# Soft-capped attention followed by a maxout layer on one core: early loads in whole rows, an earlier second stage, the last sum block and the normalisation on VectorE

## The chip, the cores and the metric

One Trainium2 chip, one of its cores. The metric is the device time of one execution in microseconds, lower is better. Times of single instructions come from one profiled execution, recorded by the hardware profiler. The kernel is written in Bass with an order of work laid out by hand: each engine runs its instructions in the order in which the program emits them, and waits on semaphores where data or a buffer is not ready.

## The reference

Attention over 8 batches, 12 heads, 448 positions, 64 columns, with a soft cap on the scores, then a layer with two products and a maximum, and an output product:

```python
scores = scale * np.matmul(q, k.transpose(0, 1, 3, 2))
scores = cap * np.tanh(scores / cap)
scores = scores - np.max(scores, axis=-1, keepdims=True)
attn = np.exp(scores)
attn = attn / (np.sum(attn, axis=-1, keepdims=True) + 1e-09)
attn_out = np.matmul(attn, v)
x = attn_out.transpose(0, 2, 1, 3).reshape(B * S, H * D)     # 3584 x 768
g = np.maximum(x @ w1, x @ w2)                               # 3584 x 1024
return g @ w_out                                             # 3584 x 768
```

The kernel writes the maximum as max(a, b) = relu(a - b) + b: it forms w1 - w2 once (`wd_sb`), and folds the "+ b" part into a premultiplied matrix w2 @ w_out (`wm_sb`). So the second stage is relu(x (w1 - w2)) @ w_out + x (w2 w_out). Preparing `wd_sb` and `wm_sb` is called M here.

## The kernel before

**Tiles.** Two heads make a pair, 48 pairs in all, six to a batch. Three pairs make a group (16 groups, g = 0 to 15), which is the unit of loading. Two pairs make a quad (24 quads, t = 0 to 23), which is the unit of the main loop. Within a quad, ab = 0 or 1 names the pair. Index i = 2t, 2t + 1 counts half quads. The 448 positions of keys are three blocks of 128 and a left block of 64; the left blocks of a pair's two heads are put together as one 128-row block.

**Attention.** `scores(t, p)` makes the scores of a quad in four parts p and puts tanh behind each on ScalarE; `ex(t, p)` is the exp on ScalarE (part 2 holds the left blocks). `pv(t, ab)` multiplies exp with v: six matmuls into `ps` for the full blocks, and one for the left one. With ab = 1 it also makes the sums of exp over the keys in `ss`, with matmuls by a matrix of ones: two 64-column ones for the left block (L340, `ones2`), and 32-column ones for the rest (L347). For quads below `NS` = 5, L347 runs over all three blocks (12 matmuls); from quad 5 on, `add` has summed the three blocks on VectorE first (`esum`, L319 and L321), and four matmuls do. VectorE copies `ps` to `U[t]` (L351, three buffers) and `ss` to `st` (L354).

**The sums' way.** `st` goes by DMA to a 32 x 56 tile `sums` (L357); `invert` takes the reciprocal on VectorE (L363) and writes it to DRAM (L365, `rec_d`); `spread` broadcasts it from there into `rec_b` (L371, two DMAs); `normalize` multiplies U by it into `xT` (L383), on GpSimd, once per pair. In the loop, spread and normalize of quad t - 2 stand in quad t.

**Loads.** Groups 0 to 3 (`NT` = 4) load k and q in rows of seven positions, 1792 bytes, and are transposed on TensorE (`transposes`); their v comes in packets of 768 and 256 bytes in four DMAs. Later groups are cast to bf16 on GpSimd (`cast`) and turned by a transposing DMA on SyncE's queue (`cross`, L268). Raw tiles have two buffers per operand. `load_w1` (SyncE), `load_w2` and `load_wo` (GpSimd, with a cast on the way) bring the weights.

**The fill.** Work of M (`turn_w2`, `premultiply`) and of the second stage (`moe(b)`, one per batch) stands in `fill_q` as generators that yield after each matmul. `F(n)` lets n of these matmuls run between the attention's steps. moe(b) has 48 first-stage matmuls (L396, 448 columns, eight groups of six, each ended by a relu on VectorE, L400), then 14 per half output tile (L408 and L411, 384 columns, ended by a copy on VectorE, L415), 84 or 112 of them. The `mm` tile, which all of the fill writes, has two PSUM buffers. F slots per quad are 44, from quad 8 on 48.

**What sets the order.** The list `todo[i]` holds loads, casts and transposing DMAs of each half quad, run by `extra(i)`; the loop over t writes out everything else. M starts at half quad `MS` = 3, `subtract` (w1 - w2, L214) is placed by MS too, and moe(0) enters the queue at the start of quad 5. SyncE's queue takes all input loads after the weights, the sums' three DMAs, the transposing DMAs and the outputs, in the order of emission.

Of the kernel before, what the change touches and what calls it, by code (L numbers as in the profile page):

```python
# [10 lines left out]
def kernel(  # L11
# [21 lines left out]
    P = 128  # L33
# [80 lines left out]
    def load(g, what, n0=0, n1=L):  # L114
        b, p = divmod(g * L, NP)
        h0, h1 = 2 * (p + n0), 2 * (p + n1)
        src = {"k": k, "q": q, "v": v}[what]
        t, m, l = raw_of(g, what)
        if g < NT and what == "v":

            x = rows(src, b, h0, h1).rearrange("(h r) c -> r h c", r=64)
            for a in range(2):
                nc.sync.dma_start(
                    out=m[64 * a : 64 * a + 64, 2 * n0 : 2 * n1, :], in_=x[:, :, NJ * D * a : NJ * D * (a + 1)]
                )
            for par in range(2):
                nc.sync.dma_start(
                    out=l[64 * par : 64 * par + 64, n0:n1, :], in_=x[:, par::2, 2 * NJ * D :]
                )
            return  # L130
        if g < NT:
            nc.sync.dma_start(
                out=t[:, n0 * S : n1 * S].rearrange("p (n c) -> p n c", c=S),
                in_=rows(src, b, h0, h1).rearrange("(n p) c -> p n c", p=P),
            )
            return
        nc.sync.dma_start(
            out=m[:, 2 * n0 : 2 * n1, :],
            in_=src[b, h0:h1, 0 : NJ * P, :].rearrange("h (p j) d -> p h (j d)", j=NJ),
        )  # L140
        if what == "q":
            nc.sync.dma_start(
                out=l[half(b), 2 * n0 : 2 * n1, :],
                in_=src[b, h0:h1, NJ * P : S, :].rearrange("h p d -> p h d"),
            )
        else:
            for par in range(2):
                nc.sync.dma_start(
                    out=l[64 * par : 64 * par + 64, n0:n1, :],
                    in_=src[b, h0 + par : h1 : 2, NJ * P : S, :].rearrange("h p d -> p h d"),  # L150
                )

    def cast(eng, g, what, n0=0, n1=L):

        b = g * L // NP
        x, m, l = raw_of(g, what)
        if what == "v":
            eng.tensor_copy(  # L158
                vp[g % 2][:, 2 * n0 : 2 * n1, :, :].rearrange("p h j d -> p h (j d)"), m[:, 2 * n0 : 2 * n1, :]
            )  # L160
            for par in range(2):
                r = slice(64 * par, 64 * par + 64)
                eng.tensor_copy(vl[g % 2][r, n0:n1, r], l[r, n0:n1, :])
            return
        if g < NT:

            x = x[:, n0 * S : n1 * S].rearrange("p (n c) -> p n c", c=S)
            if what == "q":
                eng.tensor_copy(flat(g)[:, n0:n1, Q0 : Q0 + S], x)
                return  # L170
            eng.tensor_copy(flat(g)[:, n0:n1, : NJ * P], x[:, :, : NJ * P])
            for par in range(2):
                r = slice(64 * par, 64 * par + 64)
                eng.tensor_copy(kf[g % 2][r, n0:n1, 3, r], x[r, :, NJ * P :])
            return
        o = b % 2 if what == "q" else 0
        t = (kf if what == "k" else qf)[g % 2]
        eng.tensor_copy(
            t[:, n0:n1, o : o + NJ, :].rearrange("p n j (h d) -> p n h j d", h=2),
            m[:, 2 * n0 : 2 * n1, :].rearrange("p (n h) (j d) -> p n h j d", h=2, d=D),  # L180
        )
        if what == "q":
            eng.tensor_copy(
                t[half(b), n0:n1, 3 * (1 - o), :],
                l[half(b), 2 * n0 : 2 * n1, :].rearrange("p (n h) d -> p n (h d)", h=2),
            )
        else:
            for par in range(2):
                r = slice(64 * par, 64 * par + 64)
                eng.tensor_copy(t[r, n0:n1, 3, r], l[r, n0:n1, :])  # L190
# [120 lines left out]
    def add(t, ab, step):  # L311
# [3 lines left out]
        if t not in esum:  # L315
            esum[t] = att.tile([P, 4, S], bf16, name="esum")
        d = esum[t][:, 2 * ab : 2 * ab + 2, :]
        if step == 0:
            nc.vector.tensor_add(d, e_of(t, ab, 1 if ab else 0), e_of(t, ab, 2 if ab else 1))  # L319
        else:  # L320
            nc.vector.tensor_add(d, d, e_of(t, ab, 0 if ab else 2))  # L321
# [3 lines left out]
    def pv(t, ab):  # L325
# [10 lines left out]
                )  # L336
        if ab:
            ss = pv_psum.tile([P, 512], f32, name="ss")
            for m in range(2):
                nc.tensor.matmul(  # L340
                    ss[64 * m : 64 * m + 64, :S], ones2, expo[t, 2][:, m, :], start=True, stop=False
                )
# [1 line left out]
            for j in range(nj):  # L344
                for m in range(4):
                    x = e_of(t, m // 2, j)[:, m % 2, :] if t < NS else esum[t][:, m, :]
                    nc.tensor.matmul(ss[32 * m : 32 * m + 32, :S], ones, x, start=False, stop=(j == nj - 1))  # L347
        nc.tensor.matmul(ps[:, :S], vl[g % 2][:, n, :], expo[t, 2][:, ab, :], start=False, stop=True)  # L348
        if ab == 0:
            U[t] = upool.tile([P, 2, S], f32, name="u", bufs=3)  # L350
        nc.vector.tensor_copy(U[t][:, ab, :], ps[:, :S])  # L351
        if ab:
            st = upool.tile([P, S], f32, name="st", bufs=1)
# [20 lines left out]

    xT = {}

    def normalize(t, ab, eng=nc.gpsimd):
        i = 2 * t + ab
        b, hp = divmod(i, NP)
        if i % (2 * NP) == 0:  # L380
            xT[b // 2] = xpool.tile([P, NP, 2 * S], bf16, name="xT")
        cs = slice((b % 2) * S, (b % 2 + 1) * S)
        eng.tensor_mul(xT[b // 2][:, hp, cs], U[t][:, ab, :], rec[t][:, ab, :])  # L383


    gT = {}
# [61 lines left out]
    NL = N // L  # L448
    NS = 5
    todo = [[] for _ in range(N)]  # L450

    def at(i, f, *a):
        todo[i].append((f, a))

    for g in range(2, NL):
        if g < NT:
            e = 0 if g == 2 else 1
            at(3 * g - 6 + e, load, g, "k")
            at(3 * g - 6 + e, load, g, "q")
            at(3 * g - 4 + e, load, g, "v")  # L460
            at(3 * g - 4, cast, nc.gpsimd, g, "k")
            at(3 * g - 4, cast, nc.gpsimd, g, "q")
            at(3 * g - 2, cast, nc.gpsimd, g, "v")
        else:
            e = 3 * g - g % 2
            at(e - 8, load, g, "k")
            at(e - 8 + g % 2, load, g, "q")
            at(e - 6, cast, nc.gpsimd, g, "k")
            at(e - 6, cast, nc.gpsimd, g, "q")
            at(e - 4, cross, g)  # L470
            at(e - 4, load, g, "v")
            at(e - 2, cast, nc.gpsimd, g, "v")
    at(1, load, 1, "v")
    at(2, cast, nc.gpsimd, 1, "v")
    for c, i in enumerate((3, 3, 4, 5, 6, 7)):
        todo[i].insert(c if i == 3 else 0, (load_w1, (c,)))
    MS = 3

    fill_const(nc.vector, 0)
    load(0, "k", 0, 1)  # L480
# [3 lines left out]
    load(1, "k")  # L484
    load(1, "q")
    load(0, "v")
    cast(nc.vector, 0, "k", 0, 1)
    cast(nc.gpsimd, 0, "q", 0, 1)
    fill_const(nc.gpsimd, 1)
    transposes(0)  # L490
    cast(nc.vector, 0, "k", 1, L)
    cast(nc.vector, 0, "q", 1, L)
# [7 lines left out]
    ex(0, 2)  # L500
    scores(0, 3)
    transposes(2)
    cast(nc.vector, 0, "v")
    cast(nc.gpsimd, 1, "k")
    cast(nc.gpsimd, 1, "q")
    for f in range(0, FC, 2):
        load_wo(f)
    for c in range(3):
        load_w2(c)
    for c in range(3, KC):  # L510
        load_w2(c)

    def weights(i):
# [9 lines left out]
    for t in range(NQ):  # L523
# [1 line left out]
        more = t + 1 < NQ  # L525
        more8 = 1 if t >= 8 and more else 0
        weights(i)
        if t % 3 == 2 and t > 2:
            fill_q.append(moe(t // 3 - 1))
        if more:  # L530
            scores(t + 1, 0)
        ex(t, 3)
        F(2)
        add(t, 0, 1)
        F(2)
        if i + 3 < NT * L:
            transposes(i + 3)
        F(5 + more8 if more else 0)
        if t > 4:
            spread(t - 2)  # L540
        extra(i)
        F(6 if more else 3)
        if more:
            scores(t + 1, 1)
            ex(t + 1, 0)
        pv(t, 0)
        F(8 + more8)
        F(3 if more else 0)
        if MS < i <= MS + KC:
            subtract(i - MS - 1)  # L550
        if t > 4:
            normalize(t - 2, 0)
            normalize(t - 2, 1)
        if more:
            scores(t + 1, 2)
            ex(t + 1, 1)
        weights(i + 1)
        if i + 4 < NT * L:
            transposes(i + 4)
        F(2 + more8 if more else 0)  # L560
        add(t, 1, 0)
        F(4 if more else 2)
        add(t, 1, 1)
        F(2 if more else 0)
        if t > 4:
            invert(t - 1)
        elif t > 1:
            spread(t - 2)
        extra(i + 1)
        F(3 + more8 if more else 0)  # L570
        if more:
            scores(t + 1, 3)
            ex(t + 1, 2)
        pv(t, 1)
        F(4)
        if more:
            add(t + 1, 0, 0)
        F(3 if more else 0)
        if 0 < t < 5:
            invert(t - 1)  # L580
        if 1 < t < 5:
            normalize(t - 2, 0)
            normalize(t - 2, 1)
        if MS < i + 1 <= MS + KC:
            subtract(i - MS)
    F(6)
    spread(NQ - 2)
    F(10)
    invert(NQ - 1)
    F(16)  # L590
    spread(NQ - 1)
    normalize(NQ - 2, 0)
    normalize(NQ - 2, 1)
    F(30)
    normalize(NQ - 1, 0)
    normalize(NQ - 1, 1)
    fill_q.append(moe(B - 1))
    F(10 ** 9)
# [33 lines left out]
```

## Time and profile before

| | us |
|---|---|
| median of 13 runs | 378.46 |
| lowest and highest of them | 375.65, 382.05 |
| the profiled execution | 377.91 |
| its span, first to last instruction | 376.1 |
| granted TensorE clock, mean | 0.986 |

What engine groups cost in that execution (busy us, count, mean ns):

| group | busy | count | mean |
|---|---|---|---|
| ScalarE exp L303, 1792 columns or 896 | 144.8 | 96 | 1509 |
| ScalarE tanh L296 | 124.2 | 144 | 914 |
| TensorE second stage L411, L396, L408 | 85.5, 79.2, 66.6 | 448, 384, 336 | 326, 354, 326 |
| GpSimd normalize L383, 128x448 | 58.5 | 48 | 1240 |
| VectorE esum L319, L321, 128x896 | 28.2, 29.5 | 38, 38 | 742, 777 |
| VectorE relu L400, 128x448 | 39.0 | 64 | 615 |
| TensorE sums of the left block L340 | 8.7 | 48 | 361 |

A matmul's duration here overlaps the next one's, so busy sums of TensorE overstate its work; distances between starts are the better measure. A row "engine line waited for" of a wait table gives the total, the times and the longest in microseconds.

### The profile page before, as it was taken

How to read it: one execution, taken by the hardware profiler on the slowest of the kernel's cores; microseconds unless marked ns; L12 is line 12 of the kernel's file. 1: busy time of each engine (PE TensorE's matmuls, PEld its weight loads, DVE VectorE, ACT ScalarE, POOL GpSimd, SP SyncE). 2: the span in 40 equal slices, each digit the busy share in tenths (PEclk: the TensorE clock that was granted, in tenths of full speed). 3: DMA queues.
4: the chain of work that ended last, by engine and by line, in shares of the span. 5: the costliest groups of instructions: out<-in, count | busy, mean ns of one | idle time of the engine just before them, and what ended most of it. 6: DMA issues, size and time to landing. Idle time of an engine off the chain costs nothing.

```text
span 376.1 us, 6549 instructions
## 1 busy us (share of the span) xinstructions
PE 348.2 (93%) x2492; PEld 167.7 (45%) x2492; DVE 201.5 (54%) x348; ACT 281.6 (75%) x265; POOL 148.8 (40%) x188
## 2 busy tenths in 40 slices
PE   4677887898999999999999999999999999999996
PEld 2223443342454445444444445444444454555563
DVE  4222474565665576465636755466557666533421
ACT  4999996695999989998898889988988996000000
POOL 3833137536554245615372546343643402420000
PEclk9998998998999999999999999999999999999999
DMA  7999999987779996989697959896979232332022
GB/s 269 271 217 223 300 284 234 206 159 148 209 198 203 227 252 174 211 218 250 198 245 194 250 164 248 245 243 167 249 191 244 53 113 99 108 93 84 2 84 85
DMA packets 104464, 71.56 MB, mean 190 GB/s; under 512 B 58224, under 2 KB 99440, under 8 KB 104432
## 3 DMA queue, kind: packets, MB, share of 16 engines
q1 hardware_dynamic: 102480, 67.99, 70.8%
q0 software_dynamic: 1952, 3.15, 4.5%
q8 instruction: 19, 0.31, 0.4%
q14 instruction: 13, 0.11, 0.1%
HBM read 53.48 MB, written 11.18 MB: 172 GB/s over the span
## 4 chain that ended last, share of the span: by engine, by line
PE 71%; DMA 10%; DVE 6%; ACT 4%; SPq 4%; issue 2%; POOL 2%; POOLq 0%; DVEq 0%; ACTq 0%
PE mm L411 18%; PE mm L396 17%; PE mm L408 14%; PE pv L334 7%; PE s L295 7%; PE pv L348 3%; DMA rec_b<-rec_d 3%; DMA vr<-in_v_dram 3%; DMA qkT<-kqf 2%; PE ss L347 2%; ACT tanh L296 2%; ACT expo L303 2%; PE s L290 2%; DMA qr<-in_q_dram 2%; DVE u L351 1%
## 5 line engine op out<-in xcount | busy, mean ns | idle before, releaser
L296 ACT ACTIVATE tanh<-s 128x896 bf16<-128x896 f32 x144 | 124.2, 914 | 28.8 <-PE s L295 27.6
L303 ACT ACTIVATE expo<-tanh 128x1792 bf16<-128x1792 bf16 (+1 forms) x96 | 144.8, 1509 | 0.1
L383 POOL TENSOR_TENSOR xT<-u,rec_b 128x448 bf16<-128x448 f32 x48 | 58.5, 1240 | 102.2 <-DMA rec_b<-rec_d 93.5
L411 PE MATMUL mm<-wo_sb,gT 128*128 128x384 bf16 x448 | 85.5, 326 | 0.0
L396 PE MATMUL mm<-xT,wd_sb 128*128 128x448 bf16 x384 | 79.2, 354 | 2.3 <-POOL xT L383 1.3
L351 DVE COPY u<-pv 128x448 f32<-128x448 f32 x48 | 29.9, 623 | 89.5 <-PE pv L348 78.9
L408 PE MATMUL mm<-wm_sb,xT 128*128 128x384 bf16 x336 | 66.6, 326 | 0.7 <-DVE gT L400 0.7
L411 PEld LDWEIGHTS <-gT 128*128 128x128 bf16 x448 | 43.3, 98 | 30.5 <-issue 2.6
L415 DVE COPY osb<-mm 128x384 f32<-128x384 f32 x56 | 30.9, 553 | 43.9 <-PE mm L411 43.8
L396 PEld LDWEIGHTS <-wd_sb 128*128 128x128 bf16 x384 | 37.2, 98 | 38.0 <-issue 5.4
L295 PE MATMUL s<-qkT 64*128 64x448 bf16 x288 | 43.9, 375 | 10.3 <-ACT tanh L296 3.6
L400 DVE TENSOR_SCALAR gT<-mm 128x448 bf16<-128x448 f32 x64 | 39.0, 615 | 17.2 <-PE mm L396 17.0
L408 PEld LDWEIGHTS <-xT 128*128 128x128 bf16 x336 | 32.5, 98 | 24.0 <-issue 2.7
L334 PE MATMUL pv<-expo,vp 128*64 128x448 bf16 x288 | 38.1, 374 | 0.0
L158 POOL CAST vp<-vr 128x1152 bf16<-128x1152 f32 x15 | 18.0, 1199 | 48.4 <-DMA vr<-in_v_dram 26.9
L321 DVE TENSOR_TENSOR esum<-esum,expo 128x896 bf16<-128x896 bf16 x38 | 29.5, 777 | 1.5
L319 DVE TENSOR_TENSOR esum<-expo 128x896 bf16<-128x896 bf16 x38 | 28.2, 742 | 0.0
L298 ACT ACTIVATE tanh<-s 128x896 bf16<-128x896 f32 x24 | 22.0, 916 | 5.2 <-PE s L290 4.7
L295 PEld LDWEIGHTS <-qkT 64*128 64x128 bf16 x288 | 9.6, 95 | 36.1 <-issue 30.2
L334 PEld LDWEIGHTS <-vp 128*64 128x64 bf16 x288 | 12.5, 111 | 21.9 <-issue 17.0
L232 PE MATMUL mm<-wo_sb,w2T 128*128 128x384 bf16 x96 | 18.4, 326 | 1.4 <-DVE qkT L264 1.4
L348 PE MATMUL pv<-expo,vl 128*128 128x448 bf16 x48 | 17.7, 369 | 0.0
(56 smaller groups left out, 222.2 us busy)
## 6 DMA issues: line engine op xcount, KB each, us to landing
rec_b<-rec_d SPq DMA_DIRECT2D x48, 224.0 KB
kr<-in_k_dram SPq DMA_DIRECT2D x12, 576.0 KB
qr<-in_q_dram SPq DMA_DIRECT2D x12, 576.0 KB
vr<-in_v_dram SPq DMA_DIRECT2D x12, 576.0 KB
out_dram<-osb SPq DMA_DIRECT2D x17, 384.0 KB
out_dram<-osb SPq DMA_DIRECT2D x22, 192.0 KB
osb<-in_moe_w_dram SPq DMA_DIRECT2D x6, 512.0 KB
vr<-in_v_dram SPq DMA_DIRECT2D x8, 288.0 KB
```

What stands on the lines that cost most here:

```text
L295: nc.tensor.matmul(s[:, h, :S], k0[r, j * P : (j + 1) * P], qTn[r, :])
L296: nc.scalar.activation(tanh[t, p][:, 2 * m : 2 * m + 2, :], s[:, :, :S], AF.Tanh, scale=scale / cap)
L303: nc.scalar.activation(expo[t, p], tanh[t, p][:, 0:n, :], AF.Exp, scale=float(cap))
L321: nc.vector.tensor_add(d, d, e_of(t, ab, 0 if ab else 2))
L334: nc.tensor.matmul(ps[r, :S], vp[g % 2][:, 2 * n + h, j, :], e_of(t, ab, j)[:, h, :], start=(j == 0), stop=False)
L351: nc.vector.tensor_copy(U[t][:, ab, :], ps[:, :S])
L383: eng.tensor_mul(xT[b // 2][:, hp, cs], U[t][:, ab, :], rec[t][:, ab, :])
L396: nc.tensor.matmul(ps[:, :S], wd_sb[:, c, f * P : (f + 1) * P], x[:, c, cs], start=(c == 0), stop=(c == KC - 1))
L400: nc.vector.tensor_relu(g[:, f, cs], ps[:, :S])
L408: nc.tensor.matmul(ps[:, : DM // 2], x[:, c, ts], wm_sb[:, c, hs], start=(c == 0), stop=False)
L411: nc.tensor.matmul(ps[:, : DM // 2], g[:, f, ts], wo_sb[:, f, hs], start=False, stop=(f == FC - 1))
L415: nc.vector.tensor_copy(osb[:, hs], ps[:, : DM // 2])
```

## The change

Seven things change together.

1. v of groups 0 to 3 is loaded like k and q, in 1792-byte rows with one DMA, and put in place by six casts (four of 64 partitions x 576, two of 64 x 192).
2. Loads, casts and weights of the first seven half quads are placed one by one in a table `early`; k and q of group 2 move into the opening, as do the first two pieces of w2. v of group 0 is cast in quad 0, and pv(0, 0) stands just before pv(0, 1).
3. M starts at half quad 2; `subtract` comes sooner; moe(0) enters in the middle of quad 4.
4. From group 4 on, q is loaded with k, and `cross` stands ahead of `spread`.
5. From quad 5 on the left block is summed on VectorE too (`add(t, ab, 2)`, 64 partitions x 896), and L340's two matmuls go.
6. normalize takes a quad at a time: quads below 5 with two multiplies on GpSimd, the others with one of 128 x 896 on VectorE. It stands at other places: in quad 4 early, in quads 5 and 6 ahead of scores(t + 1, 2), from quad 7 on between scores(t + 1, 3) and pv(t, 1).
7. U has four buffers. F slots per quad are 40, from quad 8 on 47, and are cut differently.

```diff
@@ load, cast @@
-        if g < NT and what == "v":
-            x = rows(src, b, h0, h1).rearrange("(h r) c -> r h c", r=64)
...
+        if what == "v" and g < NT:
+            x = x[:, : L * S].rearrange("p (n c) -> p n c", c=S)
+            for h in range(2):
+                r = slice(64 * h, 64 * h + 64)
+                for a in range(2):
+                    eng.tensor_copy(
+                        vp[g % 2][64 * a : 64 * a + 64, h::2, :, :].rearrange("p n j d -> p n (j d)"),
+                        x[r, :, NJ * D * a : NJ * D * (a + 1)],
+                    )
+                eng.tensor_copy(vl[g % 2][r, :, r], x[r, :, 2 * NJ * D :])
+            return
@@ add @@
-        if step == 0:
+        if step == 2:
+            r = slice(64 * ab, 64 * ab + 64)
+            d = esum[t][r, ab::2, :]
+            nc.vector.tensor_add(d, d, expo[t, 2][r, :, :])
+        elif step == 0:
@@ pv @@
-            for m in range(2):
+            for m in range(2 if t < NS else 0):
...
-                    nc.tensor.matmul(ss[32 * m : 32 * m + 32, :S], ones, x, start=False, stop=(j == nj - 1))
+                    nc.tensor.matmul(ss[32 * m : 32 * m + 32, :S], ones, x, start=(t >= NS), stop=(j == nj - 1))
...
-            U[t] = upool.tile([P, 2, S], f32, name="u", bufs=3)
+            U[t] = upool.tile([P, 2, S], f32, name="u", bufs=4)
@@ normalize @@
-        eng.tensor_mul(xT[b // 2][:, hp, cs], U[t][:, ab, :], rec[t][:, ab, :])
+        if t < 5:
+            for ab in range(2):
+                nc.gpsimd.tensor_mul(xT[b // 2][:, hp + ab, cs], U[t][:, ab, :], rec[t][:, ab, :])
+        else:
+            nc.vector.tensor_mul(xT[b // 2][:, hp : hp + 2, cs], U[t], rec[t])
@@ the table of loads @@
+    for g in range(NT, NL):
+        e = 3 * g - g % 2
+        crosses[(e - 4) // 2] = g
+        at(e - 8, load, g, "k")
+        at(e - 8, load, g, "q")
+        at(e - 4, load, g, "v")
+        at(e - 6, cast, nc.gpsimd, g, "k")
+        at(e - 6, cast, nc.gpsimd, g, "q")
+        at(e - 2, cast, nc.gpsimd, g, "v")
+    early = {
+        1: [(load, (1, "v"))],
+        2: [(load, (3, "k")), (load, (3, "q")), (load_w1, (0,))],
+        3: [(load_w1, (1,)), (load_w1, (2,)), (load, (2, "v"))],
+        4: [(load_w1, (3,))],
+        5: [(load_w1, (4,)), (load, (3, "v"))],
+        6: [(load_w1, (5,))],
+    }
+    for i, what in ((2, "2k"), (2, "2q"), (2, "1v"), (4, "2v"), (5, "3k"), (5, "3q"), (6, "3v")):
+        early[i].append((cast, (nc.gpsimd, int(what[0]), what[1])))
...
-    MS = 3
+    MS = 2
@@ the loop over t @@
-        F(5 + more8 if more else 0)
+        if t == 0:
+            cast(nc.vector, 0, "v")
+        F(4 + more8 if more else 0)
+        if t == 4:
+            normalize(t - 2)
+        if t in crosses:
+            cross(crosses[t])
         if t > 4:
             spread(t - 2)
         extra(i)
-        F(6 if more else 3)
+        F(5 + 2 * more8 if more else 3)
...
-        pv(t, 0)
-        F(8 + more8)
+        if t > 0:
+            pv(t, 0)
+        F(4)
+        add(t, 1, 0)
+        F(3 + more8 if more else 4)
         F(3 if more else 0)
...
-        if t > 4:
-            normalize(t - 2, 0)
-            normalize(t - 2, 1)
+        if 4 < t < 7:
+            normalize(t - 2)
...
         weights(i + 1)
+        if t == 4:
+            fill_q.append(moe(0))
...
+        add(t, 0, 2)
+        F(2 + more8 if more else 2)
+        add(t, 1, 2)
+        F(4 + more8 if more else 3)
         add(t, 1, 1)
-        F(2 if more else 0)
+        F(2 if more else 8)
...
             scores(t + 1, 3)
             ex(t + 1, 2)
+        if t > 6:
+            normalize(t - 2)
+        if t == 0:
+            pv(t, 0)
+        if t == 3:
+            spread(t - 1)
         pv(t, 1)
         F(4)
```

After the loop, F(14) stands between the last spread and normalize of quad 22, and F(24) between that and normalize of quad 23 (before: none, and F(30)).

More of the change, by code (lines that the diff above doesn't have):

```diff
@@ L118, in load @@
         t, m, l = raw_of(g, what)
-        if g < NT and what == "v":
-            x = rows(src, b, h0, h1).rearrange("(h r) c -> r h c", r=64)
[L122 to L130, printed above, removed]
         if g < NT:
@@ L375, with normalize @@
     xT = {}
-    def normalize(t, ab, eng=nc.gpsimd):
-        i = 2 * t + ab
+    def normalize(t):
+        i = 2 * t
         b, hp = divmod(i, NP)
@@ L450 @@
     todo = [[] for _ in range(N)]
+    crosses = {}
     def at(i, f, *a):
         todo[i].append((f, a))
[L455 to L476, printed above, removed]
-    MS = 3
+    for g in range(NT, NL):
[17 more added lines that the diff above has]
+        early[i].append((cast, (nc.gpsimd, int(what[0]), what[1])))
+    for i, x in early.items():
+        todo[i] += x
+    MS = 2
     fill_const(nc.vector, 0)
@@ L486 @@
     load(0, "v")
+    load(2, "k")
+    load(2, "q")
     cast(nc.vector, 0, "k", 0, 1)
@@ L489 @@
     fill_const(nc.gpsimd, 1)
+    load_w2(0)
+    load_w2(1)
     transposes(0)
@@ L502 @@
     transposes(2)
-    cast(nc.vector, 0, "v")
     cast(nc.gpsimd, 1, "k")
@@ L507 @@
         load_wo(f)
-    for c in range(3):
-        load_w2(c)
-    for c in range(3, KC):
+    for c in range(2, KC):
         load_w2(c)
@@ L527 @@
         weights(i)
-        if t % 3 == 2 and t > 2:
+        if t % 3 == 2 and t > 5:
             fill_q.append(moe(t // 3 - 1))
@@ L533 @@
         F(2)
+        if 3 < i <= 3 + KC:
+            subtract(i - 4)
         add(t, 0, 1)
@@ L545 @@
             ex(t + 1, 0)
-        pv(t, 0)
-        F(8 + more8)
-        F(3 if more else 0)
-        if MS < i <= MS + KC:
-            subtract(i - MS - 1)
-        if t > 4:
-            normalize(t - 2, 0)
-            normalize(t - 2, 1)
+        if t > 0:
[3 more added lines that the diff above has]
+        F(3 + more8 if more else 4)
+        F(3 if more else 0)
+        if 3 <= i < 3 + KC:
+            subtract(i - 3)
+        if 4 < t < 7:
+            normalize(t - 2)
         if more:
@@ L557 @@
         weights(i + 1)
+        if t == 4:
+            fill_q.append(moe(0))
         if i + 4 < NT * L:
             transposes(i + 4)
-        F(2 + more8 if more else 0)
-        add(t, 1, 0)
-        F(4 if more else 2)
-        add(t, 1, 1)
-        F(2 if more else 0)
[L565 to L570, printed above, removed]
+        add(t, 0, 2)
+        F(2 + more8 if more else 2)
+        add(t, 1, 2)
+        F(4 + more8 if more else 3)
+        add(t, 1, 1)
+        F(2 if more else 8)
+        if 1 < t < 4:
+            spread(t - 2)
+        if t > 2:
+            invert(t - 1)
+        extra(i + 1)
+        F(2 + more8 if more else 0)
         if more:
@@ L578 @@
         F(3 if more else 0)
-        if 0 < t < 5:
+        if 0 < t < 3:
             invert(t - 1)
[L581 to L585, printed above, removed]
+        if 1 < t < 4:
+            normalize(t - 2)
     F(6)
@@ L591 @@
     spread(NQ - 1)
[L592 to L596, printed above, removed]
+    F(14)
+    normalize(NQ - 2)
+    F(24)
+    normalize(NQ - 1)
     fill_q.append(moe(B - 1))
```

## The prediction

> **What bounds the kernel now.** I read the page first, then the busy times by stage, the timelines of ScalarE, SyncE, VectorE and TensorE, and last the waits. The page's first part:
>
> ```profile
> PE 348.2 (93%) x2492; PEld 167.7 (45%) x2492; DVE 201.5 (54%) x348; ACT 281.6 (75%) x265; POOL 148.8 (40%) x188
> ```
>
> TensorE is the fullest engine, but an average hides the stages. Busy time by stage (us from:to, length, then busy time and count of PE, PEld, DVE, ACT, POOL; granted clock, DMA share, GB/s):
>
> ```profile
> 30.00:42.00 12.00, 9.17 (x112) 4.56 (x112) 4.17 (x7) 11.87 (x12) 2.43 (x5) 0.86 1.09 240
> 54.00:67.00 13.00, 10.00 (x113) 5.26 (x112) 6.08 (x9) 9.95 (x10) 8.15 (x10) 0.87 1.01 240
> 67.00:82.00 15.00, 13.55 (x132) 6.55 (x131) 8.72 (x14) 11.76 (x13) 5.87 (x7) 0.99 1.04 209
> 145.70:158.00 12.30, 12.30 (x86) 6.00 (x86) 6.87 (x11) 11.76 (x13) 7.66 (x9) 1.00 0.93 241
> 247.60:261.00 13.40, 13.26 (x86) 5.92 (x86) 9.07 (x15) 11.60 (x11) 6.65 (x10) 1.00 0.70 193
> 318.60:376.00 57.40, 53.81 (x319) 30.37 (x318) 21.28 (x37) 0.00 (x0) 6.67 (x6) 1.00 0.25 80
> ```
>
> Three stages. Until about 52 us ScalarE never starves: the same tanh comes round every 11.81 us (32.38, then 44.19 in its timeline), and that is its floor per quad. From 52 to 98 us it does starve. From quad 6 on TensorE is full: the last matmuls of a quad's second pv end at 97.75 (quad 5), 313.73 (quad 22) and 320.29 (quad 23), 12.70 us per quad over 6 to 22, about 12.2 where the fill is second-stage work and 13.3 where it is the 48 first-stage matmuls. After 320 only fill is left, at full rate. In that state a TensorE microsecond saved is a microsecond, down to ScalarE's 11.81.
>
> The four quads 2 to 5 took 58.84 us (38.91 to 97.75) against 4 x 11.81 = 47.2: 11.6 us lost. The waits of the whole run name one piece of it, and the wait that matters later:
>
> ```profile
> POOL xT L383 <- DMA rec_b<-rec_d: 93.5, 22, 9.7
> ...
> DVE u L351 <- POOL xT L383: 4.0, 1, 4.0
> ```
>
> The second line is at 60.92 us: the fourth U tile needs a buffer that the first normalisation still holds, which waits for its broadcast. The first line costs nothing today: only GpSimd stands still.
>
> SyncE's timeline in quad 10 (start, length, operation):
>
> ```profile
> 150.32 0.60 SPq L357 DMA_DIRECT2D sums<-st  x1
> 151.73 1.28 SPq L371 DMA_DIRECT2D rec_b<-rec_d  x2
> 153.11 4.88 SPq L268 DMA_TRANSPOSE qkT<-kqf  x1
> ```
>
> A transpose holds SyncE's queue for 4.3 to 5.2 us (median 4.52). GpSimd's multiply, ready and waiting for that broadcast, starts at 156.66, 3.6 us after the broadcast's issue ended. TensorE in the same quad:
>
> ```profile
> 157.88 0.76 PE L334 MATMUL pv<-expo,vp 128*64 128x448 bf16 x6
> 158.47 0.36 PE L340 MATMUL ss<-expo,ones 128*64 128x448 bf16 x2
> 158.75 0.37 PE L347 MATMUL ss<-esum,ones 128*32 128x448 bf16 x4
> ```
>
> The two L340 matmuls hold TensorE from 158.47 to 158.75, 0.29 us.
>
> [...] The nearest row here, wd_sb L214 with 1024 columns, has a mean of 1268 ns[...]. [...] the esum add takes 0.61 us alone and 1.02 us at 148.34, beside a GpSimd multiply. [...]
>
> **The change, part by part**, against the profiled execution: 376.1 us of span and 1.8 around it, 377.91, which is 0.55 below the median of 378.46.
>
> *The start.* v of the first four groups goes from 768- and 256-byte packets to 1792: by the mean packet times of the first 90 us (51, 27, 95 ns) 3072 x 51 + 1536 x 27 becomes 1536 x 95 ns, over 16 engines 12.4 against 9.1 us, 3.3 us less in the stretch where the DMAs are full. SyncE issues one DMA for four. Its price is six casts in place of three; on GpSimd perhaps 1.5 us per group (64x384 takes 559 ns, 128x1152 takes 1199), hidden, because GpSimd is busy 2.4 to 8 us per quad there. Of the 11.6 us lost: the U stall in quad 3 goes with a fourth buffer (4.0); quads 2 and 4 lose 2.6, half of which I give to 40 fill matmuls in place of 44 (1.3); quad 5's 4.3 is moe(0) waiting for xT and the last wd_sb. This wait is not removed but met half a quad sooner: rec of quad 2 is inverted late in quad 3, spread behind it, 4 to 7 us to land (7.4 and 4.0 in the chain), then GpSimd's 2.3 us, just when moe(0) comes up. I leave 1.6 of it and take 2.7. Sum: -8.0. Ends: -2 if the full DMAs hand over nothing but part of the packet saving, -11.6 if all stalls go.
>
> *Fill.* F slots per quad go from 44 to 40, from quad 8 on from 48 to 47, in quad 23 from 21 to 32. M is 144 matmuls; slots from quad 1 to the middle of quad 4 are 143, so it just fits, and moe(0) gets 16 slots in quad 4. What is left after quad 23 is 139 + 160 = 299 against 135 + 160 = 295.
>
> *The left exp.* From quad 5 on two L340 matmuls go: 0.29 us per quad. VectorE gets two 64x896 bf16 adds, 0.61 us each by the esum rows, near 0.53 in pitch.
>
> *Normalisation.* From quad 7 on one 128x896 f32 multiply on VectorE, 1.1 us, in place of two GpSimd ones (1240 ns each). VectorE goes from about 7.5 to 9.5 us per quad, less some 0.3 as its adds no longer meet GpSimd's multiplies (mean 742 and 777 against 603). In a 13.4 us quad it had 9.07, so 11 there: tight, as mm has two buffers and a first-stage group is 1.1 us.
>
> *The new wait.* This multiply stands in VectorE's order ahead of the U and st copies of pv(t,1), and of each mm eviction after them; it waits for rec_b. And cross(g) is now ahead of spread(t-2) on SyncE. So the chain from one st copy to the next, in a quad with a transpose, is: sums issue 0.6, transpose 4.5, spread 1.3, landing 3.6, multiply 1.1, U copy 0.53, st 0.61, gaps 0.1: 12.3 us, plus the lag L from the end of st to the issue of sums. In the trace L is 0.03 us where SyncE is free, and 0.5 to 2.5 ahead of today's transposes, mostly because spread stood waiting for rec_d (33.7 us over 15 waits). With the transpose filling that wait I take L = 0.5: 12.8 us.
>
> Sum of the loop. Quads 9, 12, 15, 18, 21, 22 have no transpose: 0.29 + 0.17 less, of which I count 0.4: -2.4. The nine transpose quads 8, 10, 11, 13, 14, 16, 17, 19, 20 took 12.73 on average and get 12.8: +0.7. Five of these hold the first-stage matmuls, where VectorE's late evictions stop TensorE, 0.4 each: +2.0. Quad 7 (11.55, now 12.1): +0.5. Quad 23, 11 more fill matmuls less one L340: +1.5. Tail, four more matmuls: +0.7. Together +3.0, between -4.7 (waits hidden) and +15 (L of 1.5 to 2).
>
> Total -8.0 + 3.0 = -5.0: **about 373 us**, its own range 369 to 376.5.
>
> **Rivals.** *All covered, 365 us.* SyncE's queue runs earlier, rec_b lands before VectorE gets there, and TensorE keeps the whole 0.46 us: 15 x -0.46 + 2.2 for quad 23 and tail = -4.7, with -8: 365.2. For it: today in the transpose quads the broadcast mostly lands 0 to 2.3 us before pv(t,1) begins (156.66 against 157.88 in quad 10). Against it: the transpose moved ahead takes 4.5 us of that.
>
> *Slower, 385 us: VectorE waits for the broadcast behind the transpose.* If L stays at today's mean ahead of a transpose, 1.5 us, the chain is 13.8 us per transpose quad, as each late st makes the next sums late: 9 x 1.07 = +9.6, quad 7 +1.5, evictions +2.0, quad 23 and tail +2.2, the other quads gain nothing because their broadcast is already 2 to 4 us late (187.85 against pv at 183.89 in quad 12); with -8.0 that is +7.3, 385.2. It decides from L of about 1.05 us on. For it: both waits are in-order queues in one circle. Against it: fewer SyncE waits remain to make L.
>
> *No change, 378.5 us.* The start is held by the DMAs and gives -2, the loop +3 as forecast: 378.9.
>
> **How the numbers follow.** Forecast 0.38, all covered 0.24, no change 0.10, slower 0.28. 0.5% is 1.9 us, about what can be told from no change. Faster takes most of the forecast and all of the covered case, 0.58; within 0.5%, 0.13; slower 0.29. The range, 364 to 386, reaches to both ends as both signs are open; the forecast's own is 369 to 376.5.
>
> **What would show it.** Right: quad 5 ends near 90 us and not 97.75; no wait of the U copy on xT; L340 only in quads 0 to 4; VectorE waits 1 to 3 us for rec_b in the transpose quads; quads 6 to 22 near 12.7 us. Wrong: VectorE idle before the multiply by over 3 us per quad and TensorE gaps after it (slower), no such idle time (covered), or quad 5 ending after 95 us.

## The result

The changed kernel takes 390.92 us (median of 11 runs, 384.58 to 394.49), the kernel before 378.5 us (48 runs). The ratio is 1.0264, interval 1.0223 to 1.0305: slower, where 373 was forecast, with 0.29 on slower. The ratio leaves out runs more than 1.5% above the quickest of their kernel, so it is lower than the 1.033 of the two medians.

The profiled execution of the changed kernel is its quickest, 384.58 us with a span of 382.8. So what follows accounts for 6.7 us of span (382.8 less 376.1). The median lies 6 us above this execution, and that part has no profile of its own. The page's first line:

```profile
PE 347.5 (91%) x2454; PEld 165.6 (43%) x2454; DVE 243.8 (64%) x408; ACT 281.6 (74%) x265; POOL 115.0 (30%) x159
```

TensorE has 38 matmuls less and nearly the same busy time in a longer span; VectorE has 42 us more work, GpSimd 34 less. ScalarE's work is unchanged. Where the time went, by the ends of quads (last pv matmul of a quad) in both profiles:

| stretch | before, us | after, us | difference | predicted |
|---|---|---|---|---|
| start to the end of quad 5 | 97.75 | 92.68 | -5.07 | -8.0 |
| quads 6 to 22 | 215.98 | 224.90 | +8.92 | +0.8 |
| quad 23 | 6.56 | 7.96 | +1.40 | +1.5 |
| from there to TensorE's end | 52.13 | 53.78 | +1.65 | +0.7 |

The differences add up to 6.90; what comes after TensorE's end is 0.2 us shorter. The loss is in the loop. The wait table of the changed kernel has these rows (total, times, longest, us):

```profile
ACT tanh L296 <- PE s L295: 32.1, 31, 6.2
...
DVE xT L392 <- DMA rec_b<-rec_d: 23.7, 11, 5.3
...
PE mm L405 <- DVE gT L409: 8.3, 7, 4.5
...
PE mm L417 <- DVE osb L424: 3.6, 2, 2.2
```

The second row is the new wait. It is on VectorE now, where the kernel before had it on GpSimd at next to no cost. The last two are TensorE waiting for an eviction, that is for VectorE to empty an `mm` buffer. In the kernel before the longest such row of the second stage was

```profile
PE mm L408 <- DVE gT L400: 0.7, 2, 0.5
```

The place where it costs most is the multiply in quad 11 (each multiply is for the quad two before). First VectorE's timeline (start, length, operation, and in brackets how long it stood idle and for whom):

```profile
166.03 0.48 DVE L368 RECIPROCAL rec_s<-sums 32x56 f32<-32x56 f32 x1
171.80 1.09 DVE L392 TENSOR_TENSOR xT<-u,rec_b 128x896 bf16<-128x896 f32 x1 [5.29 <-DMA rec_b<-rec_d]
172.81 0.62 DVE L356 COPY u<-pv 128x448 f32<-128x448 f32 x1
173.34 0.61 DVE L359 COPY st<-ss 128x448 f32<-128x448 f32 x1
173.87 0.61 DVE L409 TENSOR_SCALAR gT<-mm 128x448 bf16<-128x448 f32 x1
```

The multiply waits 5.29 us for its broadcast. The eviction of a first-stage group (L409), ready by 170, is third in the row behind it. Now TensorE:

```profile
167.81 1.49 PE L405 MATMUL mm<-xT,wd_sb 128*128 128x448 bf16 x7
169.23 0.55 PE L295 MATMUL s<-qkT 64*128 64x448 bf16 x4
169.72 0.36 PE L405 MATMUL mm<-xT,wd_sb 128*128 128x448 bf16 x1
174.54 4.30 PE L405 MATMUL mm<-xT,wd_sb 128*128 128x448 bf16 x15 [4.46 <-DVE gT L409]
178.78 0.55 PE L295 MATMUL s<-qkT 64*128 64x448 bf16 x4
```

Both `mm` buffers are full at 170, and TensorE stands still for 4.46 us. The next 15 matmuls take 4.30 us, not the 2.8 they take elsewhere. The second part of quad 13's scores, behind them, comes late, and ScalarE starves for 6.2 us (the first wait row's longest). And SyncE, which shows why the broadcast was late:

```profile
158.90 0.61 SPq L362 DMA_DIRECT2D sums<-st  x1
161.48 1.12 SPq L444 DMA_DIRECT2D out_dram<-osb  x2
162.71 4.02 SPq L268 DMA_TRANSPOSE qkT<-kqf  x1
166.82 1.34 SPq L376 DMA_DIRECT2D rec_b<-rec_d  x2
```

From the end of quad 10's st copy (158.87) to the multiply it is 12.93 us: sums, an output that itself waited 1.9 us for an eviction on VectorE, the transpose, the broadcast, 3.65 us to land. The broadcast is quad 9's, but it stands behind quad 10's sums in SyncE's order.

Adding up the distances between starts of matmuls that exceed 0.6 us (less 0.2 each) from 92 us on gives 1.6 us of TensorE stops before and 14.4 after. The four multiplies in quads 10, 11, 16 and 20 waited 3.9, 5.3, 4.1 and 2.8 us; the stops of 1.5, 4.6, 2.4 and 2.2 us that go with them are 10.7 of the 14.4.

### The profile page after: what moved, and what is told of

Same layout as the page of the kernel before. It is cut to its first block, busy times and chain, and to the rows that moved or that the text cites. A ratio compares the mean times of both kernels' runs of the same rounds, so it can differ in the third digit from the quotient of the medians.

```text
span 382.8 us, 6452 instructions
## 1 busy us (share of the span) xinstructions
PE 347.5 (91%) x2454; PEld 165.6 (43%) x2454; DVE 243.8 (64%) x408; ACT 281.6 (74%) x265; POOL 115.0 (30%) x159
## 4 chain that ended last, share of the span: by engine, by line
PE 38%; DMA 25%; DVE 13%; SPq 10%; ACT 6%; POOL 5%; issue 3%; DVEq 0%; POOLq 0%; ACTq 0%
PE mm L405 9%; DMA rec_b<-rec_d 9%; PE mm L420 8%; DMA rec_d<-rec_s 7%; PE mm L417 6%; SPq L268 5%; DMA kr<-in_k_dram 5%; PE pv L339 4%; DMA qr<-in_q_dram 4%; PE s L295 3%; SPq L376 3%; ACT tanh L296 3%; PE mm L232 3%; ACT expo L303 3%; POOL kqf L178 2%
## 5 line engine op out<-in xcount | busy, mean ns | idle before, releaser
L405 PE MATMUL mm<-xT,wd_sb 128*128 128x448 bf16 x384 | 81.1, 357 | 9.5 <-DVE gT L409 8.3
L417 PE MATMUL mm<-wm_sb,xT 128*128 128x384 bf16 x336 | 67.5, 328 | 3.8 <-DVE osb L424 3.6
L424 DVE COPY osb<-mm 128x384 f32<-128x384 f32 x56 | 30.8, 551 | 25.5 <-PE mm L420 25.2
L409 DVE TENSOR_SCALAR gT<-mm 128x448 bf16<-128x448 f32 x64 | 39.2, 616 | 11.0 <-PE mm L405 10.7
L158 POOL CAST vp<-vr 128x1152 bf16<-128x1152 f32 x12 | 15.0, 1254 | 98.3 <-DMA vr<-in_v_dram 88.0
L392 DVE TENSOR_TENSOR xT<-u,rec_b 128x896 bf16<-128x896 f32 x19 | 20.3, 1067 | 23.7 <-DMA rec_b<-rec_d 23.7
L324 DVE TENSOR_TENSOR esum<-expo 128x896 bf16<-128x896 bf16 x38 | 30.8, 812 | 0.0
L326 DVE TENSOR_TENSOR esum<-esum,expo 128x896 bf16<-128x896 bf16 x38 | 26.3, 693 | 1.6
L322 DVE TENSOR_TENSOR esum<-esum,expo 64x896 bf16<-64x896 bf16 x38 | 24.1, 635 | 0.7
L178 POOL CAST kqf<-kr 128x1152 bf16<-128x1152 f32 x12 | 14.2, 1185 | 29.6 <-DMA kr<-in_k_dram 28.7
```

The lines of the kernel that those rows point to most:

```text
L405: nc.tensor.matmul(ps[:, :S], wd_sb[:, c, f * P : (f + 1) * P], x[:, c, cs], start=(c == 0), stop=(c == KC - 1))
L409: nc.vector.tensor_relu(g[:, f, cs], ps[:, :S])
L417: nc.tensor.matmul(ps[:, : DM // 2], x[:, c, ts], wm_sb[:, c, hs], start=(c == 0), stop=False)
L424: nc.vector.tensor_copy(osb[:, hs], ps[:, : DM // 2])
```

## The experiments

Theory A: the multiply in VectorE's order waits for a late broadcast, and everything behind it waits too. Theory B: VectorE simply has too much to do. Each ratio is to the kernel before, measured beside the experiment (medians 379.12, 379.65 and 379.31 us); "stops" are counted as above.

**Taking the wait away, keeping the work.** The multiply reads U twice; the normalisation is left out from quad 5 on, and nobody waits for the broadcast.

```diff
-            nc.vector.tensor_mul(xT[b // 2][:, hp : hp + 2, cs], U[t], rec[t])
+            nc.vector.tensor_mul(xT[b // 2][:, hp : hp + 2, cs], U[t], U[t])
```

> The changed kernel with its VectorE multiply taking U times U in place of U times the reciprocal's broadcast, so from quad 5 on the normalisation is left out; the broadcast is still sent, nobody waits for it. Same place, same operation, same VectorE work. Theory A: the whole loss goes: 366 to 374 us, ratio 0.965 to 0.987, TensorE gaps under 8 us. Theory B: nothing changes, 386 to 391, ratio 1.02 to 1.03.

371.41 us, ratio 0.9808 (0.9747 to 0.9869). Stops 2.7 us. VectorE's work is the same, 244.7 us for 243.8. By stage, over quads 11 and 12 (columns as in the prediction):

```profile
155.00:167.00 12.00, 12.00 (x79) 5.70 (x79) 8.59 (x16) 11.84 (x12) 1.78 (x3) 1.00 0.89 226
167.00:180.00 13.00, 13.00 (x82) 5.78 (x79) 10.98 (x18) 11.82 (x12) 5.87 (x8) 1.00 0.74 200
```

VectorE is busy for 10.98 of 13 us in the second row and TensorE never stops. B falls: the work can be borne, the wait can't.

**The same multiply, later in the order.**

```diff
+        if t > 7:
+            normalize(t - 3)
         weights(i)
...
-        if t > 6:
-            normalize(t - 2)
...
+    normalize(NQ - 3)
```

(the last line stands behind the loop)

> The changed kernel, but from quad 7 on the multiply stays on VectorE and moves behind the end of its quad: the multiply of quad t - 3 stands at the top of quad t, some 2 to 4 us later in VectorE's order. VectorE's work is the same. Theory A: most broadcasts have landed by then, VectorE's idle time before the multiply falls to under 8 us: 368 to 377 us, ratio 0.975 to 0.995. Theory B: same work, same time, 386 to 391.

375.59 us, ratio 0.9897 (0.9876 to 0.9919). Stops 8.1 us. VectorE's wait for rec_b is nearly gone, as A expects:

```profile
DVE xT L392 <- DMA rec_b<-rec_d: 1.9, 3, 0.7
```

It stays 4 us behind the run without the wait; 4.9 us of its stops are five waits for the relu's eviction (L409), and what held that up was not followed further.

**The same multiply, sooner.**

```diff
-        if 4 < t < 7:
+        if t > 4:
             normalize(t - 2)
...
-        if t > 6:
-            normalize(t - 2)
```

> The changed kernel with the VectorE multiply some 3 us sooner in every quad, ahead of scores(t + 1, 2), where quads 5 and 6 have it. Theory A: the broadcast lands no sooner, so the wait is longer by about 3 us in most quads from 7 to 22, and the time goes up with it: 395 to 425 us, ratio 1.045 to 1.12. Theory B: same work in another order: 385 to 392, ratio 1.015 to 1.035.

434.56 us, ratio 1.1454 (1.1381 to 1.1528), more than A expected.

```profile
ACT tanh L296 <- PE s L295: 84.5, 38, 8.1
...
DVE xT L392 <- DMA rec_b<-rec_d: 47.8, 14, 6.4
```

The wait doubles. But the row was also longer behind it: the left-block adds now stand behind the multiply, and pv's sums wait for them (19.5 us in 12 waits for L322, 5.7 in 7 for L326). So its size isn't that of the wait alone; its direction is.

**The multiply on GpSimd.**

```diff
-        if t < 5:
+        if t < NQ:
             for ab in range(2):
                 nc.gpsimd.tensor_mul(xT[b // 2][:, hp + ab, cs], U[t][:, ab, :], rec[t][:, ab, :])
```

> The changed kernel, but all normalising multiplies are on GpSimd, two per quad, at the changed kernel's places. Theory A: GpSimd can wait for the broadcast without stopping an eviction; the early gain and the saved left-block matmuls remain: 366 to 373 us, ratio 0.97 to 0.985, TensorE gaps after quad 6 under 4 us in all. Theory B: also faster, as 20.3 us of VectorE work go, but 24 us of left-block adds stay: 374 to 382.

372.68 us, ratio 0.982 (0.9784 to 0.9857). Stops 4.6 us, where under 4 was expected. In the same quad 11 as above, GpSimd's timeline, then VectorE's:

```profile
169.50 2.61 POOL L390 TENSOR_TENSOR xT<-u,rec_b 128x448 bf16<-128x448 f32 x2 [8.33 <-DMA rec_b<-rec_d]
```

```profile
165.36 0.48 DVE L368 RECIPROCAL rec_s<-sums 32x56 f32<-32x56 f32 x1
167.03 0.62 DVE L356 COPY u<-pv 128x448 f32<-128x448 f32 x1 [1.19 <-PE pv L353]
167.57 0.61 DVE L359 COPY st<-ss 128x448 f32<-128x448 f32 x1
168.10 0.61 DVE L409 TENSOR_SCALAR gT<-mm 128x448 bf16<-128x448 f32 x1
```

The broadcast is as late as ever, 8.33 us of waiting on GpSimd, but U is copied at 167.03, when pv is done, and the eviction goes out at 168.10. Its waits of 73.5 us in all from 80 to 330 us cost next to nothing there.

**One part alone, on the kernel before.** From quad 7 on one multiply on VectorE ahead of pv(t, 1), nothing else (the two last quads, behind the loop, too).

```diff
-        if t > 4:
+        if 4 < t < 7:
             normalize(t - 2, 0)
             normalize(t - 2, 1)
...
             ex(t + 1, 2)
+        if t > 6:
+            normalize2(t - 2)     # tensor_mul on VectorE, 128 x 896
         pv(t, 1)
...
-    normalize(NQ - 2, 0)
-    normalize(NQ - 2, 1)
+    normalize2(NQ - 2)
     F(30)
-    normalize(NQ - 1, 0)
-    normalize(NQ - 1, 1)
+    normalize2(NQ - 1)
```

> The kernel before with one part of the change: from quad 7 on its multiply is one on VectorE, ahead of pv(t, 1), with the spread still ahead of the transpose and the left block on TensorE. Theory A (a multiply in VectorE's order that waits for the broadcast stops the evictions behind it, and TensorE with them): this part alone makes the kernel slower, 386 to 397 us, ratio 1.02 to 1.05, with TensorE gaps of over 8 us in all where the kernel before has 1.6. Theory B (VectorE's load): 20 us more on an engine that is 54% busy: 379 to 383, ratio 1.00 to 1.012.

389.57 us, ratio 1.0269 (1.0206 to 1.0333), stops 11.3 us, 3.2 of them after quad 23.

```profile
DVE xT L383 <- DMA rec_b<-rec_d: 20.6, 7, 4.9
```

This part alone loses what the whole change loses; what the other parts gain together with the multiply on GpSimd (0.982) doesn't show in the whole. Here the spread still stands ahead of the transpose.

**The order on SyncE.**

```diff
-        if t in crosses:
-            cross(crosses[t])
         if t > 4:
             spread(t - 2)
+        if t in crosses:
+            cross(crosses[t])
         extra(i)
```

> The changed kernel, but the broadcast of the reciprocals is issued ahead of the transposing DMA again. Theory A (VectorE's multiply waits for a broadcast that stands behind the transpose, and everything behind it in VectorE's queue waits too): the broadcast lands some 4.5 us sooner in the transpose quads; VectorE's idle time before the multiply falls from 23.7 us to under 10, TensorE's gaps with it, and the time is 375 to 381 us, ratio to before 0.99 to 1.005. Theory B (VectorE has too much work, 243.8 us for 201.5; the wait is incidental): its work is the same, so the time stays at 386 to 391, ratio 1.02 to 1.03.

390.2 us, ratio 1.0254 (1.0195 to 1.0313). This is what was expected of B and not of A. As the first experiment excludes B, it is a part of A that falls: the transpose ahead of the broadcast isn't the cause.

```profile
DVE xT L392 <- DMA rec_b<-rec_d: 17.1, 7, 5.1
POOL xT L390 <- DMA rec_b<-rec_d: 15.6, 5, 4.0
```

VectorE waits less often, but its long waits are as long: they have moved to the quads without a transpose (5.12 us ahead of the multiply in quad 9, 3.86 in quad 12, 2.37 in 15, 3.59 in 18). The run before this one, with the same order on SyncE, has its longest waits in such quads too (4.94 in 12, 3.83 in 15, 4.26 in 18). Scores now wait 4.4 us for transposes that start later, and the stops are 18.1 us. So the order on SyncE decided which quad's broadcast was late, and not whether one was. That rec_d comes late there behind transpose and loads is likely, not shown.

**VectorE relieved of the left-block adds.** `add(t, ab, 2)` taken out, L340's two matmuls back.

```diff
-        add(t, 0, 2)
-        add(t, 1, 2)
...
-            for m in range(2 if t < NS else 0):
+            for m in range(2):
...
-                    nc.tensor.matmul(ss[32 * m : 32 * m + 32, :S], ones, x, start=(t >= NS), stop=(j == nj - 1))
+                    nc.tensor.matmul(ss[32 * m : 32 * m + 32, :S], ones, x, start=False, stop=(j == nj - 1))
```

> The changed kernel, but the left block is summed by the two 64-column matmuls again, and VectorE's two adds of 635 ns per quad go. Theory A: the wait for the broadcast remains, TensorE gets 0.29 us per quad more work: 386 to 395 us, ratio 1.02 to 1.045. Theory B: 24 us less VectorE work make it faster: 377 to 384, ratio 0.995 to 1.015.

393.68 us, ratio 1.036 (1.0316 to 1.0404). Less work on VectorE and a slower kernel, against B. The same edit on the kernel with GpSimd multiplies:

> The kernel with all multiplies on GpSimd, and the left block summed by TensorE's two matmuls again: what the left block's move is worth once the wait is gone. If the 0.29 us per quad are worth their face value on a full TensorE, 19 x 0.29 = 5.5 us more than the kernel with the multiplies on GpSimd: 376 to 380, ratio 0.992 to 1.002. If VectorE's 24 us of adds cost TensorE as much in late evictions as they save: 371 to 374, ratio 0.978 to 0.988.

377.14 us, ratio 0.9916 (0.9881 to 0.9951). It lies between the two expectations. GpSimd's multiplies alone gave 0.982 and, in a later run, 0.9883, so the left block's move to VectorE looks worth between 0.3 and 1% once the wait is gone, where its face value was 1.5%. Against the later run the intervals overlap, so a gain is likely and not certain.

**The U buffer of the start.** The kernel before with `bufs=4` for U.

```diff
-            U[t] = upool.tile([P, 2, S], f32, name="u", bufs=3)
+            U[t] = upool.tile([P, 2, S], f32, name="u", bufs=4)
```

> The kernel before with a fourth U buffer and nothing else. If the prediction's 4.0 us for the U copy that waited for the first normalisation are worth their face value, quad 5 ends 4 us sooner than 97 to 98 and the time is 373 to 376, ratio 0.985 to 0.993. If the start is held elsewhere (weights, full DMAs, moe(0)'s xT), the 4 us go into the next wait: 377 to 380, ratio 0.997 to 1.003.

379.04 us, ratio 0.9981 (0.9951 to 1.0012): no difference is shown, and 4 us would have been 1.1%. In its profile quad 3 does get shorter, 13.02 us for 16.57, but quads 4 and 5 take 1.4 us longer (quad 5 17.00 for 16.09), and the end of quad 5 moves only from 97.75 to 96.14. Quad 0 ended 2.0 us later and quad 1 was 1.5 shorter, which the edit doesn't reach: one profile of each can't say more of this stretch.

**More fill for the quicker kernel.** One, then two more matmuls per quad from quad 5 on, on top of the GpSimd multiplies (the same edit at one `F(3 ...)`, then at two), and that kernel again.

```diff
-        F(3 if more else 0)
+        F((4 if t > 4 else 3) if more else 0)
```

> The kernel with all multiplies on GpSimd and one more fill matmul per quad from quad 5 to 22, 18 in all, which are then missing at the end. In its quads that run at ScalarE's floor (11.85 us) they are free, and the tail is 18 x 0.165 = 3 us shorter: 369 to 372, ratio 0.974 to 0.982. If they only lengthen the quads: the same as the kernel without them, 371 to 375.

> The same with two more fill matmuls per quad, 36 in all, so 49 per quad from quad 8 on, which is a little more than the second stage brings (48.7 per quad). If the light quads still have room: 367 to 371, ratio 0.968 to 0.98. If TensorE is full, or moe has to wait for xT because it has caught up: 371 to 376.

> The kernel with all multiplies on GpSimd, once more, beside the two with more fill, on the same chip. Ratio 0.978 to 0.986 as in its first run if its gain is the chip's and not a draw.

Ratios 0.9902 (0.9864 to 0.994) with one more, 0.9843 (0.9804 to 0.9881) with two, 0.9883 (0.9832 to 0.9934) with none. The intervals overlap; no gain from the fill is shown. All three are quicker than both kernels; the medians are 375.37, 372.6 and 374.51 us.

## Why the prediction was wrong

The likeliest case named the right wait and priced it too low.

*Shown right.* The wait of the multiply for the broadcast, and that it stops evictions and TensorE, was put down with its place ("The new wait" and the case "Slower, 385 us"). Three runs show it: without the wait 0.9808, later 0.9897, and alone on the kernel before 1.0269. The U wait on xT is gone; the sums of the left block run on TensorE in quads 0 to 4 only (10 matmuls). The multiply, put at 1.1 us (by columns, L214 of the kernel before, 1268 ns for 1024, gives an estimate of 1.11), measured 1067 ns on average. Quad 23 (+1.40 for +1.5) and the cast of a group's v on GpSimd (4 x 0.74 + 2 x 0.35 = 3.7 us for 1.9, predicted 1.5 more) came out near their price.

*The step that failed* is "VectorE's late evictions stop TensorE, 0.4 each: +2.0". TensorE's stops grew by 12.8 us (14.4 less 1.6), and 1.8 us more went in 11 fill matmuls that ran at half rate after a stop. I took a chain's average against a quad's average; but one late broadcast does not cost the difference of the two. It fills both `mm` buffers, and then TensorE stands for all the rest: 4.46 us in one piece. The matching term "Quads 9, 12, 15, 18, 21, 22 ... -2.4" fell with it. Those six quads took 14.46 us on average, 12.97 before, since the stop of a multiply at the end of one quad shows in the next; quad 12 alone took 18.78. The transpose quads, forecast at 12.8, took 12.81 on average, by luck: they ran from 11.84 to 15.70, for a late broadcast came in some and not in all.

*The deciding point of the slower case was wrong too*, though its 385.2 lies beside this execution's 384.58. I had it decide by the lag L from st to sums, above 1.05 us. L was 0.03 us ahead of all nine transposes. The chain was longer in some quads for another reason: from the end of st to the multiply it was 9.5 to 12.9 us, where 10.6 was reckoned, and in the four of 12 us or more (quads 10, 11, 16 and 20) outputs stand between sums and the transpose. In quad 11 the output waited 1.9 us for an eviction (VectorE's L424 at 160.90) that was itself behind quad 10's late multiply (156.72). So there was a circle, as that case said, but it closed through the outputs. And the transpose's place ahead of the spread, which I made part of the mechanism, gains nothing when undone (1.0254).

*The start* brought -5.07 for -8.0, and here a term was left out. Quads 2 to 5, for which the -8.0 was reckoned, took 50.79 us for 58.84, 8.05 less. But quad 1 ended at 41.89 and not at 38.91, 2.98 later, because ScalarE now waits there. The tanh at the same place in its order, before and after:

```profile
29.04 1.73 ACT L296 ACTIVATE tanh<-s 128x896 bf16<-128x896 f32 x2
32.01 1.73 ACT L296 ACTIVATE tanh<-s 128x896 bf16<-128x896 f32 x2 [2.92 <-PE s L295]
```

It waits for the first scores of quad 2. On TensorE they stand behind pv(0, 0) and pv(0, 1), which now run one behind the other from 25.46 to 31.4. The five other profiled runs with the same first six quads have this wait too, 2.5 to 2.9 us. The prediction put the move of pv(0, 0) at nothing. The move was not undone alone, so this is read from the traces. That 8.05 meets 8.0 so closely is luck: in those five runs quads 2 to 5 took 51.0 to 52.6 us and quad 5 ended at 93.42 to 95.11. In the run with only the multiply changed, which has the start of the kernel before, they took 56.3, and quad 5 ended at 96.70. The largest term, 4.0 us for the U buffer, did not show as such in the single run with four buffers. Which of the other edits made the gain is not settled; they weren't tried one by one.

*Left open.* Why the median is 6 us above the profiled execution. The mean granted clocks of the 11 runs lie between 0.970 and 0.990, and two stops of the profiled one came with 3.4 us each at a granted clock of 0.5 (below), which would fit; but a run of 389.06 us had the same 0.990 as the quickest, and there is no profile of a median run. Two kernels that are close to this one, profiled at 392.06 us (the order on SyncE) and 394.14 us (without the left-block adds), had 18.1 and 18.2 us of stops, so more stops are a candidate. Also, in the kernel with GpSimd multiplies, the case "all covered, 365 us" was not reached (372.7 and 374.5): its start gave -3.5 us in the profile and its loop -3.2, from the same table of ends, with 4.6 us of stops left.

## What to carry to other kernels

A wait is cheap or dear by what stands behind it in its engine's queue. Before moving an operation to a faster engine (here 1.07 us for twice 1.24), look up whether it is the one that waits: 93.5 us of waiting on GpSimd cost next to nothing, while 23.7 us on VectorE came with 12.8 us more of TensorE stops. If such an operation has to go there, put it behind the point where its data has surely landed, even a stage later (0.9897 here, for 1.0264), and count a stall with the number of buffers that it fills and not as an average.

## What the runs showed of the hardware

After the 4.82 us between the starts at 169.72 and 174.54 in the changed kernel, TensorE ran at half rate: six distances between matmuls of 448 columns were 0.373 us, and from 177.35 on they were 0.19; the clock records show 0.5 granted from 173.81 to 177.22, 3.4 us. A second stretch at 0.5, from 242.07 to 245.49, began during a wait of 2.23 us, while a wait of 2.03 us at 292 brought none. The row of the first stretch:

```profile
166.00:182.00 16.00, 11.54 (x65) 4.60 (x64) 8.28 (x14) 9.06 (x10) 5.67 (x8) 0.89 0.85 214
```

In the run with the multiply sooner, whose stops came to 53.3 us and whose mean granted clock was 0.949, 39 fill matmuls ran so (distances of 0.3 to 0.45 us) and cost 6.3 us more. And a VectorE add of 64 partitions x 896 (L322) took 616 ns on average where nothing ran on GpSimd beside it, one of 128 partitions 614 or 624 (L324, L326): half the partitions saved nothing.
